# Sums of x on GpSimd between the weight sums, visits kept apart by time, and quad 7 on SP's queue

## The chip, the cores and the metric

The kernel runs on one core of one Trainium2 chip. The metric is the device time of one execution in microseconds (us); smaller is better. Four runs of the kernel before gave 420.64, 421.08, 419.64 and 419.05 us, with a median of 420.14 us. A profile of one execution of each kernel is at hand. Its engines are PE (the matrix engine), PEld (PE's weight loads), DVE (vector), ACT (scalar), POOL (GpSimd) and SP (which only issues DMAs here).

## The reference

Sigmoid attention on 8 batches of 12 heads, 448 positions and head size 64, followed by a gated feed-forward block on the 3584 resulting rows of width 768, with an inner width of 1536:

```python
scores = scale * np.matmul(q, k.transpose(0, 1, 3, 2)) - np.log(S)
attn = 1.0 / (1.0 + np.exp(-scores))          # no softmax: no sum over keys
x = np.matmul(attn, v)                        # then heads side by side: (3584, 768)
g = x @ w_gate
silu = g * (1.0 / (1.0 + np.exp(-g)))
out = (silu * (x @ w_val)) @ w_out
```

## The kernel before, in words

**Attention** is done in 24 *quads*: quad n holds four heads of batch n // 3. Each quad has seven chunks of 64 keys (per head). For one chunk, PE computes the scores of four heads with four small matmuls (L230), ACT applies the sigmoid and writes the tile `pt` (L248, or L245 where the tile is done in halves), and after the seventh chunk PE multiplies by v (`pv`, 28 matmuls at L262). The product lies in PSUM and is copied to two tiles `xT` (L271, L276 on DVE, partly L279 or L284 on ACT). Three quads make the six `xT` tiles of one batch.

**The first feed-forward product** of batch b is `ffn1(b, f)` for f = 0..11: 12 matmuls with 128x448 results (L296), the gate (L314 on ACT, L316 and L320 on DVE) and the tile `hT`. For the last two batches, 6 and 7, it is done another way: `ffn1_pair(j)`, six times, makes seven block products in place of eight (a Strassen-Winograd form, L403), in the order 1, 2, 6, 5, 7, 3, 4. It needs sums of blocks of the weights (`wS`, made by `wx_sums` on POOL, L357, 8 instructions per j) and sums of blocks of x (`xS`, made by `x_sums(i)` for i = 0, 1, 2, L371, 4 instructions each). `x_sums(i)` takes quad 18 + i of batch 6 and quad 21 + i of batch 7, so it can run only when quad 21 + i has its `xT`. Products 6, 5, 7 and 4 of every pair read `xS`.

**The second product** takes two batches at a time: `ffn2` (24 matmuls, L614) for one block of rows, and `ffn2_group(pb, g)` (42 matmuls, L556) for two, again with seven block products, on sums `S` of `hT` (L515) and sums `wT` of w_out (L484). Inside a group, DVE must copy a PSUM bank out (`snap`, L567) before PE may add the next product to it: product 6 is queued behind the snap of product 1.

**PSUM** is a ring of four tiles of two banks; every score tile, `pv`, `ffn1` and group takes the next one.

**The order** of all engines is written out by the program, and no scheduler changes it. A list `units` (L635 on) holds the feed-forward work with estimated durations (FU1 = 2.26 us for an `ffn1`, 3.9 for an `ffn2`, 6.83 for a group). A list `visits` holds the attention work: each quad is visited twice, (n, 0) for chunks 0 to 3 and (n, 4) for chunks 4 to 6; `vtime` gives each visit a due time, spaced by FAST. The loop at L851 walks through the units, adds up their durations in `tcur` and puts a visit ahead of a unit when it is due and when more than one unit stands between it and the visit before (`since > 1`); after LAST, the end of `ffn1(5, 11)`, that second condition is dropped. `pv` of a quad is done in the visit after its second one. A dictionary `plan` (L826) says what is issued behind a visit: `fetch(n)` (q, k and v of quad n loaded through POOL's DMA queue), `casts(n)` (q and k to bf16 on POOL, L181), `trans(n)` (two transposing DMAs on SP's queue, L188), and the sums. `ready(n)` is `casts(n)` and `trans(n)` together. SP's queue also carries the stores of the result (L526). All queues are in order.

`load` puts a quad's q and k into one of four staging tiles; the `casts` of two quads earlier free the tile.

Of the kernel before, what the change touches and what calls it, by code (L numbers as in the profile page):

```python
# [21 lines left out]
def kernel(  # L22
# [10 lines left out]
    nc = tc.nc  # L33
    ctx.enter_context(tc.manual_schedule())

    B, H, S, D = q.shape
# [3 lines left out]
    NJ = H // 4  # L40
    NP = H // 2
    NF = DFF // 128
    NQ = B * NJ
# [9 lines left out]
    stg = ctx.enter_context(tc.tile_pool(name="stg", bufs=4))  # L53
    c16 = ctx.enter_context(tc.tile_pool(name="c16", bufs=4))
# [108 lines left out]
    def load(n, which, eng=None):  # L163
        ramp = 2 * n + (1 - which)
        st = (
            stg.tile([128, 2, S], FP32, tag=f"R{ramp}", bufs=1, name=f"st{which}_{n}")
            if ramp < NR else stg.tile([128, 2, S], FP32, tag="stg", name=f"st{which}_{n}")
        )
        (eng or nc.sync).dma_start(out=st, in_=src_of(n, which))
        qkv_st[(n, which)] = st  # L170

    def load_v(n):
        t = v16p.tile([128, 2, S], FP16, tag="v16", name=f"v16_{n}")
        nc.gpsimd.dma_start(out=t, in_=src_of(n, 2))  # L174
        v16[n] = t
# [157 lines left out]
    def wx_sums(j, room):  # L333

        s = j // FW * 2
        cs = slice(j % FW * 128, j % FW * 128 + 128)
        for kind, w16 in enumerate((wg16, wv16)):
            if room == "stg":
                t = stg.tile([128, 2, S], FP32, tag="stg", name=f"wS{kind}_{j}").bitcast(FP16).rearrange("p a b -> p (a b)")
                t = [t[:, i * 384:(i + 1) * 384] for i in range(4)]  # L340
            else:
                t = []
                for i in range(2):
                    if room == "c16":
                        u = c16.tile([128, C, 2, D], BF16, tag="c16", name=f"wS{kind}_{j}_{i}").bitcast(FP16)
                        u = u.rearrange("p c h d -> p (c h d)")
                    else:
                        u = ptp.tile([128, 2, S], FP16, tag="pt", name=f"wS{kind}_{j}_{i}").rearrange("p a b -> p (a b)")
                    t += [u[:, :384], u[:, 384:768]]
            t = [u.rearrange("p (i n) -> p i n", i=NP // 2) for u in t]  # L350
            a11, a12 = w16[s][:, 0::2, cs], w16[s][:, 1::2, cs]
            a21, a22 = w16[s + 1][:, 0::2, cs], w16[s + 1][:, 1::2, cs]
            if j == 0 and kind == 0:

                nc.gpsimd.tensor_copy(out=t[0][:, 0, :1], in_=hT[(LB // 2 - 1, NF - 1)][:, 1, :1])
            for n, a, b, op in ((1, a21, a22, ADD), (2, t[0], a11, SUB), (3, a11, a21, SUB), (4, a12, t[1], SUB)):
                nc.gpsimd.tensor_tensor(out=t[n - 1], in0=a, in1=b, op=op)  # L357
                wS[(kind, n, j)] = t[n - 1]

    def x_sums(i):  # L360

        t = []
        for n in range(2):
            if i < 2:
                u = v16p.tile([128, 2, S], FP16, tag="v16", name=f"xS{i}_{n}")
            else:
                u = ptp.tile([128, 2, S], FP16, tag="pt", name=f"xS{i}_{n}")
            t += [u[:, 0, :], u[:, 1, :]]
        b11, b12, b21, b22 = (xT[(LB + h, 2 * i + p)] for p in range(2) for h in range(2))
        for n, a, b, op in ((3, b22, b12, SUB), (2, t[2], b11, ADD), (1, b12, b11, SUB), (4, b21, t[1], SUB)):  # L370
            nc.vector.tensor_tensor(out=t[n - 1], in0=a, in1=b, op=op)  # L371
            xS[(n, i)] = t[n - 1]

    def f32_of(tag):
# [290 lines left out]
    FIRST = f1_end[0] - 5.0  # L665
    LAST = f1_end[LB - 1]
    QN = 2 * NJ
    SLOW = 12.2
    FAST = (LAST - 5.5 - (FIRST + 3.5 + 3 * SLOW)) / (NQ - 2 - QN - 3)
    at_end = {(NQ - 2, 4): LAST, (NQ - 1, 0): LAST + FU2, (NQ - 1, 4): LAST + FU2 + FU3}  # L670
    tiles = [(n, c) for n in range(NJ, NQ) for c in range(C)]
    visits = [tiles[:2], tiles[2:4]]
    for i in range(0, len(tiles), C):
        visits += [tiles[i:i + 4], tiles[i + 4:i + C]] if i else [tiles[4:C]]
    vtime = []
    for grp in visits:
        n, c = grp[0]
        b, j = divmod(n, NJ)
# [5 lines left out]
            vtime.append(at_end.get((n, c), FIRST + 3.5 + min(at, 3) * SLOW + max(at - 3, 0) * FAST) - 0.01)  # L684

    def attn_step(group, pvs, how):
        done = list(pvs)
        for part in (group[:2], group[2:]):
            scs = [(n, c, qk_tile(n, c)) for n, c in part]
            rest = [pv(pvs.pop(0), how) for _ in range(len(pvs))]  # L690
            for i, (n, c, sc) in enumerate(scs):

                sig_tile(n, c, sc, split=len(group) == 4 and part[0] == group[0] and i == 1)
            for f in rest:
                f()
        for n in done:
            if n // NJ == B - 1:
                x_sums(n % NJ)

    NPE = 2 * NJ  # L700

# [31 lines left out]
    def fetch(n):  # L733
        load(n, 0, G)
        load(n, 1, G)
        load_v(n)

    def w_out(i):
# [79 lines left out]
    for f, Df in enumerate(early):  # L818
# [7 lines left out]
    plan = {  # L826
        (3, 2): ((casts, 5), (post.append, 4)),
        (3, 4): ((post.append, 5),),
        (4, 0): ((fetch, 6),),
        (4, 4): ((ready, 6),),  # L830
        (5, 4): ((fetch, 7), (w_out, 0)),
        (6, 0): ((ready, 7), (w_out, 1)),
        (6, 4): ((fetch, 8), (w_out, 2)),
        (7, 0): ((ready, 8), (w_out, 3)),
        (7, 4): ((fetch, 9),),
# [8 lines left out]
        if n + 3 < NQ:  # L844
            plan[(n, 4)] += ((fetch, n + 3),)

    plan[(NQ - 1, 0)] = tuple((partial(wx_sums, room=r), j) for j, r in enumerate(("stg", "stg", "c16")))
    plan[(NQ - 1, 4)] = ((partial(wx_sums, room="pt"), 3),)


    seq = []  # L851
    tcur = 3 * FU1
    since = 99
    was, was_args = ffn1, (0, 2)
    for dur, fn, args in units:
        if visits and tcur >= vtime[0] and not (was is ffn1 and was_args[1] == 0) and (vtime[0] < FIRST + 4 or since > 1 or tcur > LAST - 0.1):
# [14 lines left out]
    for fn, args, how in seq:  # L871
        if fn is None:
            pvs, pend = pend, []
            attn_step(args, pvs, how)
            for n, c in args:
                for act, of in plan.get((n, c), ()):
                    act(of)
                if c == C - 1:
                    pend.append(n)
            while post:  # L880
                trans_pe(post.pop())
            continue
# [37 lines left out]
```

## Time and profile before

| what | value |
|---|---|
| median of 4 runs | 420.14 us |
| profiled execution | 420.64 us |
| its span, first to last instruction | 418.3 us |
| PE busy | 401.1 us (96%) |
| DVE, ACT, POOL busy | 266.2, 232.0, 157.6 us |
| mean granted clock of PE | 0.990 |

The profiled execution took 2.34 us more than its span; that part lies outside the first and last instruction. A row of a timeline is: start in us, duration in us, engine, line, operation, tiles, shapes, count, and in brackets the idle time before it with what ended it. A row of a group is the same without a start, and behind the bar the busy time in us, the mean of one in ns, and the idle time before. A row of a stretch gives for each engine its busy time and, in brackets, the number of instructions, then the granted PE clock (1.00 is full), the share of the DMA engines and GB/s. Matmuls overlap (one is shown with about 0.35 us, though the next starts after 0.16 to 0.19 us), so "PE busy" hides short losses; starts of rows are the better measure.

### The profile page before, as it was taken

What the parts mean: (1) busy time and instruction counts of PE and PEld (TensorE: products, weight loads), DVE (VectorE), ACT (ScalarE), POOL (GpSimd) and SP (SyncE); (2) the same over time, 40 slices, a digit from 0 to 9 for tenths busy, and PEclk for the clock granted to TensorE, in tenths of its full rate; (3) what the DMA queues carried; (4) which work ended last, traced back from release to release, by engine and by line L of the source; (5) the groups of instructions that cost most, each with busy time, mean ns of one, the idle gap of its engine ahead of it and who ended that gap; (6) DMA issues with size and microseconds to landing.
All of it is one profiled execution on the core that took longest, in us unless ns stands there. A gap on an engine that the chain in (4) does not pass through costs nothing. (4 is left out here: it accounts for less than half of the span.)

```text
span 418.3 us, 8017 instructions
## 1 busy us (share of the span) xinstructions
PE 401.1 (96%) x3158; PEld 207.5 (50%) x3158; DVE 266.2 (64%) x474; ACT 232.0 (55%) x333; POOL 157.6 (38%) x194
## 2 busy tenths in 40 slices
PE   7799999999999999999999999999987799999995
PEld 3444544445565444454555444445444455555553
DVE  2636647678854545777655455677896646886753
ACT  5976885745415677677304667667772136566100
POOL 3628153334330633330003243200299607996000
PEclk9899999999999999999999999999999989999999
DMA  8999999997779986573226979332012330000125
GB/s 271 244 262 235 213 211 227 120 197 201 204 142 242 205 198 148 100 114 90 55 78 144 250 178 191 55 42 45 3 38 57 96 77 1 1 2 0 39 77 148
DMA packets 59844, 54.38 MB, mean 130 GB/s; under 512 B 35744, under 2 KB 53280, under 8 KB 59808
## 3 DMA queue, kind: packets, MB, share of 16 engines
q0 software_dynamic: 18880, 30.94, 33.9%
q1 hardware_dynamic: 40496, 22.62, 26.9%
q8 instruction: 24, 0.39, 0.4%
q10 hardware_dynamic: 432, 0.33, 0.3%
q14 instruction: 12, 0.10, 0.1%
HBM read 47.19 MB, written 11.01 MB: 139 GB/s over the span
## 5 line engine op out<-in xcount | busy, mean ns | idle before, releaser
L248 ACT ACTIVATE pt<-ps_D,sb_t 128x896 f16<-128x896 f32 x148 | 140.3, 1011 | 79.2 <-PE ps_D L230 78.9
L296 PE MATMUL ps_D<-xT,wg 128*128 128x448 f16 x432 | 95.3, 353 | 0.1
L296 PE MATMUL ps_D<-xT,wv 128*128 128x448 f16 x432 | 94.8, 352 | 0.0
L316 DVE TENSOR_TENSOR t<-ps_D,s 128x448 f16<-128x448 f32 x72 | 44.8, 622 | 62.0 <-ACT s L314 61.9
L181 POOL CAST c<-st 128x896 bf16<-128x896 f32 x41 | 38.2, 944 | 112.9 <-DMA T<-c 60.6
L296 PEld LDWEIGHTS <-wv 128*128 128x128 f16 x432 | 42.2, 98 | 39.5 <-issue 0.4
L296 PEld LDWEIGHTS <-wg 128*128 128x128 f16 x432 | 39.4, 98 | 45.1 <-issue 12.4
L314 ACT ACTIVATE s<-ps_D 128x448 f16<-128x448 f32 x72 | 39.7, 551 | 39.8 <-PE ps_D L296 20.9
L320 DVE SCALAR_TENSOR_TENSOR hT<-ps_D,t 128x448 f16<-128x448 f32 x72 | 45.0, 625 | 7.5
L230 PE MATMUL ps_D<-T,T 64*64 64x448 bf16 x644 | 44.9, 360 | 3.3 <-ACT pt L248 1.2
L556 PE MATMUL ps_D<-wT,S 128*128 128x384 f16 x198 | 35.6, 337 | 5.0 <-DVE osb L567 5.0
L556 PEld LDWEIGHTS <-S 128*128 128x128 f16 x264 | 26.4, 100 | 23.4 <-issue 7.1
L262 PE MATMUL ps_D<-pt,v 64*64 64x448 f16 x672 | 37.1, 358 | 0.5 <-DMA v<-in_v_dram 0.5
L567 DVE TENSOR_SCALAR osb<-ps_D 128x384 f32<-128x384 f32 x43 | 24.0, 557 | 19.6 <-PE ps_D L556 19.3
L174 POOL DMA_DIRECT2D v<-in_v_dram x24 | 17.6, 733 | 49.3 <-PE ps_D L230 47.6
L230 PEld LDWEIGHTS <-T 64*64 64x64 bf16 x644 | 15.2, 106 | 26.6 <-issue 19.4
L271 DVE CAST xT<-ps_D 128x448 f16<-128x448 f32 x24 | 15.0, 624 | 19.0 <-PE ps_D L262 18.7
L573 DVE SCALAR_TENSOR_TENSOR osb<-ps_D,osb 128x384 f32<-128x384 f32 x33 | 18.4, 558 | 13.1 <-PE ps_D L556 12.9
L262 PEld LDWEIGHTS <-v 64*64 64x64 f16 x672 | 19.8, 109 | 13.7 <-issue 1.4
L556 PEld LDWEIGHTS <-hT 128*128 128x128 f16 x198 | 18.9, 98 | 14.2 <-issue 2.1
L276 DVE CAST xT<-ps_D 64x448 f16<-64x448 f32 x40 | 24.9, 621 | 0.6
L614 PE MATMUL ps_D<-wo,hT 128*128 128x384 f16 x144 | 24.2, 326 | 0.5 <-ACT pt L248 0.5
(78 smaller groups left out, 431.0 us busy)
## 6 DMA issues: line engine op xcount, KB each, us to landing
out_dram<-osb SPq DMA_DIRECT2D x52, 192.0 KB, 2.9
st<-in_q_dram POOLq DMA_DIRECT2D x20, 448.0 KB, 4.5
st<-in_k_dram POOLq DMA_DIRECT2D x20, 448.0 KB, 5.6
v<-in_v_dram POOLq DMA_DIRECT2D x24, 224.0 KB, 7.1
wg<-in_moe_w_gate_dram POOLq DMA_DIRECT2D x4, 576.0 KB, 12.0
wv<-in_moe_w_val_dram POOLq DMA_DIRECT2D x4, 576.0 KB, 12.6
wo<-in_moe_w_out_dram POOLq DMA_DIRECT2D x4, 576.0 KB, 10.9
st<-in_q_dram SPq DMA_DIRECT2D x3, 448.0 KB, 7.7
```

Of the source, the lines that this page charges most:

```text
L181: eng.tensor_copy(out=t.rearrange("p c h d -> p h c d"), in_=st.rearrange("p h (c d) -> p h c d", c=C))
L230: nc.tensor.matmul(out=sc[w * 64:(w + 1) * 64, h2, :S], lhsT=kt[r, w * 64:(w + 1) * 64], rhs=qt[r, :, w * 64:(w + 1) * 64], start=True, st ...
L248: nc.scalar.activation(out=pt, in_=sc[:, :, :S], func=SIGM, bias=sb_t, scale=qkscale)
L262: nc.tensor.matmul(out=P[g:g + 64, h2, :S], lhsT=vt[r, h2, c * D:(c + 1) * D], rhs=pt[r, h2, :], start=(c == 0), stop=(c == C - 1),)
L276: done = [nc.vector.tensor_copy(out=o, in_=i) for o, i in halves[how:]]
L296: nc.tensor.matmul(out=D.t[:, i, :S], lhsT=(wg16, wv16)[i][f // FW][:, pr, cs], rhs=xT[(b, pr)], start=(pr == 0), stop=(pr == NP - 1),),
L314: D.read(nc.scalar.activation(out=s16, in_=D.t[:, 0, :S], func=SIGM), 0)
L316: D.read(nc.vector.tensor_tensor(out=t1, in0=D.t[:, 0, :S], in1=s16, op=MULT), 0)
L320: nc.vector.scalar_tensor_tensor(out=hT[(b // 2, f)][:, b % 2, :], in0=D.t[:, 1, :S], scalar=HSC, in1=t1, op0=MULT, op1=MULT),
L556: nc.tensor.matmul(out=D.t[:, bank, :hw], lhsT=l, rhs=B_(i), start=(first and i == 0), stop=(i == HF - 1), skip_group_check=True,),
L567: nc.vector.tensor_scalar(out=o, in0=D.t[:, bank, :hw], scalar1=HREC, scalar2=None, op0=MULT), bank
L614: nc.tensor.matmul(out=D.t[:, half, :hw], lhsT=h[:, m * 128:(m + 1) * 128], rhs=wo16[f // FW][:, f % FW, half * hw:(half + 1) * hw], start ...
```

## The change

The change has four parts.

1. `x_sums` runs on POOL and not on DVE. Its three calls move from the place behind the `pv` to places between the weight sums: behind visit (22, 4) come `wx_sums(0)` and `x_sums(0)`, behind (23, 0) come `x_sums(1)` and `wx_sums(1)`, and behind the last `pv` come `x_sums(2)`, `wx_sums(2)` and `wx_sums(3)`. Tiles that hold the sums are of the same pools as before.
2. A visit is now held back until 3.8 us of estimated unit time have gone by since the visit before, in place of more than one unit, and the exception after LAST is gone.
3. FAST is computed from `LAST - 6.7` and not `LAST - 5.5`, which makes it 11.04 and not 11.13 us per quad. Parts 2 and 3 together move most visits from (9, 4) on by a unit or two towards the start.
4. q and k of quad 7 are loaded on SP's queue (`fetch_sp`) and not on POOL's; its v stays on POOL.

```diff
@@ x_sums
         for n, a, b, op in ((3, b22, b12, SUB), (2, t[2], b11, ADD), (1, b12, b11, SUB), (4, b21, t[1], SUB)):
-            nc.vector.tensor_tensor(out=t[n - 1], in0=a, in1=b, op=op)
+            nc.gpsimd.tensor_tensor(out=t[n - 1], in0=a, in1=b, op=op)
@@
-    FAST = (LAST - 5.5 - (FIRST + 3.5 + 3 * SLOW)) / (NQ - 2 - QN - 3)
+    FAST = (LAST - 6.7 - (FIRST + 3.5 + 3 * SLOW)) / (NQ - 2 - QN - 3)
@@ attn_step
-        done = list(pvs)
...
-        for n in done:
-            if n // NJ == B - 1:
-                x_sums(n % NJ)
@@
+    def fetch_sp(n):
+        load(n, 0)
+        load(n, 1)
+        load_v(n)
@@ plan
-        (5, 4): ((fetch, 7), (w_out, 0)),
+        (5, 4): ((fetch_sp, 7), (w_out, 0)),
...
-    plan[(NQ - 1, 0)] = tuple((partial(wx_sums, room=r), j) for j, r in enumerate(("stg", "stg", "c16")))
-    plan[(NQ - 1, 4)] = ((partial(wx_sums, room="pt"), 3),)
+    wx_stg = partial(wx_sums, room="stg")
+    plan[(NQ - 2, 4)] = ((wx_stg, 0), (x_sums, 0))
+    plan[(NQ - 1, 0)] = ((x_sums, 1), (wx_stg, 1))
@@ the loop over units
-    since = 99
+    last = -9.0
-        if visits and tcur >= vtime[0] and not (...) and (vtime[0] < FIRST + 4 or since > 1 or tcur > LAST - 0.1):
+        if visits and tcur >= vtime[0] and not (...) and (vtime[0] < FIRST + 4 or tcur - last > 3.8):
...
-            since = 0
-        seq.append((fn, args, not visits and since == 1))
+            last = tcur
+        seq.append((fn, args, not visits and tcur - last > 3.8))
...
-        since += dur > 0.0
@@ behind the last visit
             for n in pend:
                 pv(n, 2 if how else 0)
-                if how:
-                    x_sums(n % NJ)
+            if how:
+                x_sums(2)
+                wx_sums(2, "c16")
+                wx_sums(3, "pt")
```

First place: DVE between the last block of `ffn2` of batches 4 and 5 (L627 copies it out) and the start of their first group (L567 and L573 copy a group's products out). Before:

```order
L627 TENSOR_SCALAR osb<-ps_D_101 128x384 x2
L271 CAST xT_2_4161<-ps_D_102 128x448
L276 CAST xT_3_4163<-ps_D_102 64x448
L371 TENSOR_TENSOR xS_1_4184<-xT_3_4163,xT_2_4161 128x448
L371 TENSOR_TENSOR xS_0_4183<-xS_1_4184,xT_2_3698 128x448
L371 TENSOR_TENSOR xS_0_4183<-xT_2_4161,xT_2_3698 128x448
L371 TENSOR_TENSOR xS_1_4184<-xT_3_3700,xS_0_4183 128x448
L567 TENSOR_SCALAR osb<-ps_D_100 128x384
L573 SCALAR_TENSOR_TENSOR osb<-ps_D_100,osb 128x384
```

The same place of the changed kernel:

```order
L627 TENSOR_SCALAR osb<-ps_D_101 128x384 x2
L271 CAST xT_2_4172<-ps_D_102 128x448
L276 CAST xT_3_4174<-ps_D_102 64x448
L567 TENSOR_SCALAR osb<-ps_D_100 128x384
L573 SCALAR_TENSOR_TENSOR osb<-ps_D_100,osb 128x384
```

The four sums have left; the snap of the group (L567) now stands directly behind the casts of quad 22. The same happens in the third group, and the four sums of quad 21 leave the place behind the second visit's casts.

Second place: POOL, from the last weight sum of j = 0. Before, the first weight sum of j = 1 came next; now:

```order
L357 TENSOR_TENSOR wS_0_4090<-wv_0_107,wS_0_4090 128x384
L371 TENSOR_TENSOR xS_1_4096<-xT_1_3998,xT_0_3996 128x448
L371 TENSOR_TENSOR xS_0_4095<-xS_1_4096,xT_0_3458 128x448
L371 TENSOR_TENSOR xS_0_4095<-xT_0_3996,xT_0_3458 128x448
L371 TENSOR_TENSOR xS_1_4096<-xT_1_3460,xS_0_4095 128x448
L371 TENSOR_TENSOR xS_1_4195<-xT_3_4174,xT_2_4172 128x448
L371 TENSOR_TENSOR xS_0_4194<-xS_1_4195,xT_2_3620 128x448
L371 TENSOR_TENSOR xS_0_4194<-xT_2_4172,xT_2_3620 128x448
L371 TENSOR_TENSOR xS_1_4195<-xT_3_3622,xS_0_4194 128x448
L357 TENSOR_TENSOR wS_1_4200<-wg_1_104 128x384
```

Eight sums of x stand between the weight sums of j = 0 and j = 1; the last four stand behind those of j = 1 and ahead of those of j = 2.

Third place: ACT around the end of `ffn1(5, 11)`, with the gates of `ffn1(5, 10)` and `ffn1(5, 11)` (L314) and the sigmoids of quad 22 (L248, L245). Before, all seven score tiles of quad 22 follow the two gates:

```order
L314 ACTIVATE s_3976<-ps_D_100 128x448
L314 ACTIVATE s_3993<-ps_D_102 128x448
L248 ACTIVATE pt<-ps_D_101,sb_t 128x896
L245 ACTIVATE pt<-ps_D_99,sb_t 128x448 x2
L284 CAST xT_1_4042<-ps_D_100 64x448
L248 ACTIVATE pt<-ps_D_102,sb_t 128x896
L248 ACTIVATE pt<-ps_D_101,sb_t 128x896
L248 ACTIVATE pt<-ps_D_99,sb_t 128x896
L248 ACTIVATE pt<-ps_D_100,sb_t 128x896
L248 ACTIVATE pt<-ps_D_102,sb_t 128x896
```

Now the first four stand ahead of the two gates, and three behind them:

```order
L248 ACTIVATE pt<-ps_D_100,sb_t 128x896
L245 ACTIVATE pt<-ps_D_102,sb_t 128x448 x2
L248 ACTIVATE pt<-ps_D_99,sb_t 128x896
L248 ACTIVATE pt<-ps_D_100,sb_t 128x896
L314 ACTIVATE s_4034<-ps_D_102 128x448
L314 ACTIVATE s_4055<-ps_D_101 128x448
L248 ACTIVATE pt<-ps_D_99,sb_t 128x896
L248 ACTIVATE pt<-ps_D_100,sb_t 128x896
L248 ACTIVATE pt<-ps_D_102,sb_t 128x896
```

Visits (22, 0) and (22, 4) no longer stand back to back; two units lie between them.

More of the change, by code (lines that the diff above doesn't have):

```diff
@@ L845 @@
             plan[(n, 4)] += ((fetch, n + 3),)
-    plan[(NQ - 1, 0)] = tuple((partial(wx_sums, room=r), j) for j, r in enumerate(("stg", "stg", "c16")))
-    plan[(NQ - 1, 4)] = ((partial(wx_sums, room="pt"), 3),)
+    wx_stg = partial(wx_sums, room="stg")
+    plan[(NQ - 2, 4)] = ((wx_stg, 0), (x_sums, 0))
+    plan[(NQ - 1, 0)] = ((x_sums, 1), (wx_stg, 1))
     seq = []
     tcur = 3 * FU1
-    since = 99
+    last = -9.0
     was, was_args = ffn1, (0, 2)
     for dur, fn, args in units:
-        if visits and tcur >= vtime[0] and not (was is ffn1 and was_args[1] == 0) and (vtime[0] < FIRST + 4 or since > 1 or tcur > LAST - 0.1):
+        if visits and tcur >= vtime[0] and not (was is ffn1 and was_args[1] == 0) and (vtime[0] < FIRST + 4 or tcur - last > 3.8):
             seq.append((None, visits.pop(0), 0 if fn is ffn1 else 1))
             vtime.pop(0)
-            since = 0
-        seq.append((fn, args, not visits and since == 1))
+            last = tcur
+        seq.append((fn, args, not visits and tcur - last > 3.8))
         was, was_args = fn, args
-        since += dur > 0.0
         tcur += dur
```

## The prediction

> **What bounds the kernel now.** I read the page's busy times first, then the stretches, then PE's waits, then timelines of the stretch that stands out.
>
> ```profile
> PE 401.1 (96%) x3158; PEld 207.5 (50%) x3158; DVE 266.2 (64%) x474; ACT 232.0 (55%) x333; POOL 157.6 (38%) x194
> ```
>
> PE is the bound, so only time in which PE does not issue is to be had. Where that lies, three stretches show:
>
> ```profile
> 30.00:300.00 270.00, 269.90 (x2230) 138.08 (x2232) 172.56 (x317) 163.56 (x226) 81.54 (x102) 1.00 0.75 152
> 300.00:345.00 45.00, 38.11 (x303) 20.63 (x296) 31.19 (x50) 18.69 (x25) 30.05 (x33) 0.96 0.24 62
> 345.00:414.00 69.00, 68.86 (x383) 37.10 (x380) 48.32 (x85) 27.11 (x56) 33.13 (x36) 1.00 0.13 34
> ```
>
> From 30 to 300 us PE is idle for 0.1 us, from 345 on for 0.14 us. Only the 45 us between hold loss: 6.89 us idle and a clock of 0.96. PE's waits name the cause of most of it:
>
> ```profile
> PE ps_D L556 <- DVE osb L567: 5.0, 2, 2.8
> ```
>
> Twice a group's product 6 waited for the snap (L567). DVE's rows show what stood ahead of the snap:
>
> ```profile
> 311.12 0.62 DVE L276 CAST xT<-ps_D 64x448 f16<-64x448 f32 x1
> 311.83 0.50 DVE L371 TENSOR_TENSOR xS<-xT,xT 128x448 f16<-128x448 f16 x1
> ...
> 314.29 1.09 DVE L371 TENSOR_TENSOR xS<-xT,xS 128x448 f16<-128x448 f16 x1
> 315.30 0.55 DVE L567 TENSOR_SCALAR osb<-ps_D 128x384 f32<-128x384 f32 x1
> ```
>
> The four sums of quad 22 fill DVE from 311.83 to 315.30, 3.5 us, with the snap directly behind: without them it starts at 311.8, or when product 1 is there.
>
> **The terms.** Busy time hides pipelined losses, so I take them from starts. The measure without a stall comes from visits and groups that had none:
>
> ```profile
> 281.87 0.76 PE L230 MATMUL ps_D<-T,T 64*64 64x448 bf16 x12
> 282.57 1.31 PE L296 MATMUL ps_D<-xT,wg 128*128 128x448 f16 x6
> 283.71 1.30 PE L296 MATMUL ps_D<-xT,wv 128*128 128x448 f16 x6
> ...
> 287.21 0.57 PE L230 MATMUL ps_D<-T,T 64*64 64x448 bf16 x8
> ...
> 289.42 1.31 PE L296 MATMUL ps_D<-xT,wg 128*128 128x448 f16 x6
> ```
>
> A visit of three tiles takes 282.57 - 281.87 = 0.70 us, one of four tiles with a `pv` 289.42 - 287.21 = 2.21 us, and six matmuls of an `ffn1` 283.71 - 282.57 = 1.14 us (0.19 each). Now quads 22 and 23:
>
> ```profile
> 299.40 0.57 PE L230 MATMUL ps_D<-T,T 64*64 64x448 bf16 x8
> ...
> 304.43 4.06 PE L614 MATMUL ps_D<-wo,hT 128*128 128x384 f16 x24 [0.52 <-ACT pt L248]
> 308.42 0.57 PE L230 MATMUL ps_D<-T,T 64*64 64x448 bf16 x8
> ```
>
> *Visits of quad 22.* (22, 0) and (22, 4), back to back, take 304.43 - 299.40 = 5.03 us, against 2.21 + 0.70: 2.12 lost. PE waits for the ring, which ACT empties:
>
> ```profile
> 302.47 4.60 ACT L248 ACTIVATE pt<-ps_D,sb_t 128x896 f16<-128x896 f32 x5
> ```
>
> Five tiles take 4.60 us, 0.92 each, and PE makes one in 0.23 (0.70 for three). Apart by two `ffn1`, the spacing of the 281.87 and 287.21 rows, which had no stall, each costs its 0.70 and 2.21: gain 2.12. Bounds: 2.12, or 0 if the queue on ACT only moves on to (23, 0). But (22, 4) needs 3 x 0.92 us of ACT and the `ffn2` behind it gives 3.99 us (304.43 to 308.42), so I take 2.12.
>
> ```profile
> 310.94 2.12 PE L556 MATMUL ps_D<-wo,hT 128*128 128x384 f16 x12
> 315.90 3.08 PE L556 MATMUL ps_D<-wT,S 128*128 128x384 f16 x18 [2.83 <-DVE osb L567]
> ```
>
> *Visit (23, 0)* takes 310.94 - 308.42 = 2.52, 0.31 over 2.21. Its third tile needs the ring place that L627 empties on DVE, and the changed order still has six sums of hT (L515) on DVE there; so I leave this 0.31 in.
>
> *The two snaps.* Matmuls of the undisturbed second group give the pace, and behind them the third group begins:
>
> ```profile
> 323.53 3.09 PE L556 MATMUL ps_D<-wT,S 128*128 128x384 f16 x18
> ...
> 326.45 1.14 PE L556 MATMUL ps_D<-wo,S 128*128 128x384 f16 x6
> ...
> 328.50 1.52 PE L262 MATMUL ps_D<-pt,v 64*64 64x448 f16 x28
> ...
> 329.95 2.12 PE L556 MATMUL ps_D<-wo,hT 128*128 128x384 f16 x12
> ```
>
> ```profile
> 334.20 4.76 PE L556 MATMUL ps_D<-wT,S 128*128 128x384 f16 x18 [2.12 <-DVE osb L567]
> ...
> 338.80 1.14 PE L556 MATMUL ps_D<-wo,S 128*128 128x384 f16 x6
> ```
>
> From 323.53 to 326.45 it is 2.92 us for 18, 0.162 each; 12 take 1.95. First group: 315.90 - 310.94 - 1.95 = 3.01 lost. Third group: 334.20 - 329.95 - 1.95 = 2.30 lost. Both go with the sums: ahead of the snap only the casts stay, which by the rows end at 311.74, 1.2 us before product 2 is issued (310.94 + 1.95). What would be late next is the bank of product 2, with its own `put`, which the second group (323.53 on) shows without a wait.
>
> *The clock.* The 18 matmuls from 334.20 take 338.80 - 334.20 = 4.60 where 2.92 is the pace: 1.68 lost. The stretches show why:
>
> ```profile
> 314.15:317.57 3.42, 1.67 (x11) 1.02 (x11) 2.75 (x5) 0.00 (x0) 3.37 (x4) 1.00 0.00 0
> 331.22:334.63 3.41, 1.29 (x9) 0.68 (x7) 3.27 (x6) 0.00 (x0) 1.60 (x2) 1.00 0.30 91
> 334.63:338.05 3.42, 3.42 (x13) 1.66 (x11) 0.95 (x3) 0.00 (x0) 0.00 (x0) 0.50 0.00 0
> ```
>
> After a stretch with 1.29 us of PE work the clock is halved for 3.4 us; after one with 1.67 it is not. With the second wait gone no such stretch is left: gain 1.68. The Trainium skill ("TensorE: Matmul & The Clock Gate", "What's actually happening") says otherwise: the clock halves after at least one idle window of about 3.4 us. PE was never idle that long, so by it this half clock has another cause and the 1.68 may stay. The row at 331.22 speaks for the wait.
>
> *The sums on POOL.* The trace has no sum of x on POOL. The nearest rows are the weight sums, also two f16 tiles to one:
>
> ```profile
> L357 POOL TENSOR_TENSOR wS<-wg,wS 128x384 f16<-128x384 f16 x4 | 3.9, 986 | 0.0
> ```
>
> ```profile
> 300.84 0.25 POOL L355 COPY wS<-hT 128x1 f16<-128x1 f16 x1 [33.26 <-DVE S L515]
> ```
>
> ```profile
> 320.58 0.91 POOL L357 TENSOR_TENSOR wS<-wv 128x384 f16<-128x384 f16 x1
> ...
> 331.77 1.06 POOL L357 TENSOR_TENSOR wS<-wv,wS 128x384 f16<-128x384 f16 x1
> ```
>
> By width, 448/384, a sum costs between 0.91 x 1.17 = 1.06 and 1.06 x 1.17 = 1.24; I take 1.06, since DVE has no two-input sums in most of that time. Twelve add 12.7 us to POOL. Is that covered? POOL starts at L355, about 1.4 us after the visit behind `ffn1(5, 11)` begins (300.84 - 299.40). That visit is now (22, 4). Behind it PE does 0.70, `ffn2` 3.99, (23, 0) 2.52, three groups of 42 x 0.162 = 6.8, (23, 4) 0.70 and the last `pv` 1.45 (329.95 - 328.50): 29.8 us. Product 6 of the first pair comes after 12 matmuls at 0.19, 2.3 us later, and its third matmul first needs `xS` of quad 23: 32.4 - 1.4 = 31 us from L355. POOL needs for the copy, 16 weight sums at 0.986 and ten sums of x: 0.25 + 15.8 + 10.6 = 26.7, or 29.6 at the upper ends 1.06 and 1.24. So it is in time by 1.4 to 4.3 us, and the path pays nothing. The weight sums of j = 2 and 3 follow and are needed two and three pairs (42 x 0.19 = 8 us each) after the first pair's.
>
> *The other moved visits* (from (9, 4) on) lie in the 270 us where PE is full: the same matmuls in another order, 0. A visit that moves by two `ffn1` comes 4 x 1.14 = 4.6 us sooner, and what covers that is the lead of its quad's transposes over its scores; without it PE would wait as in the first rival below.
>
> *Quad 7 on SP.* SP issues its two loads behind both transposes of quad 6. The casts of quad 6's k and of quad 7's k, on POOL, and what a load of this size took on SP:
>
> ```profile
> 51.45 0.94 POOL L181 CAST c<-st 128x896 bf16<-128x896 f32 x1 [0.22 <-DMA st<-in_k_dram]
> ...
> 60.84 0.94 POOL L181 CAST c<-st 128x896 bf16<-128x896 f32 x1 [2.41 <-DMA st<-in_k_dram]
> ```
>
> ```profile
> st<-in_k_dram SPq DMA_DIRECT2D x3, 448.0 KB, 9.1
> ```
>
> k of quad 7 landed by 60.84. On SP it is issued near 54.4 (an estimate: the transpose behind the cast that ends at 52.4, 1.2 us of issue as in the row of L188 below, and two load issues) and lands between 60.8, if the DMA engines set the end, and 54.4 + 9.1 = 63.5. Behind the cast of k wait POOL's loads of quad 8, so its transposes slip by 0 to 2.7 us:
>
> ```profile
> L188 SPq DMA_TRANSPOSE T<-c x2: 1222/1227/1232, 73.2 to 74.6; - x2
> ...
> DMA to landing us min/median/max: 4.9/10.9/16.9
> ```
>
> ```profile
> 94.91 0.57 PE L230 MATMUL ps_D<-T,T 64*64 64x448 bf16 x8
> ```
>
> The second lands at 74.6 + 16.9 = 91.5, and PE wants it at 94.9: a lead of 3.4 us, so 0.7 is left at the worst end. Cost 0.
>
> **Sum.** 2.12 + 3.01 + 2.30 + 1.68 = 9.11. The profiled execution took 420.64 us for a span of 418.3; with 9.1 less that is **411.5 us**. It lay 0.5 above the median of the four runs, 420.14; part of that may be the half clock, which need not fall in every run, so the gain on the median may be nearer 8.6.
>
> **Rivals.**
> - *Quad 8 comes late* (0.13). For: the lead may fall to 0.7, and the second transpose of quad 8 took 16.9 us where the first took 4.9, so it stood behind other transfers. Against: the bytes are the same. If the loads land 2 us later than my upper end, PE waits 1.3 us and may earn a half clock of 1.7 on top: 412.8 to 414.5.
> - *The half clock stays* (0.08), by another cause than the wait: 411.5 + 1.7 = 413.2.
> - *Sums late by a little* (0.07): at 1.4 us per sum of x and 1.06 per weight sum, POOL needs 0.25 + 17.0 + 14 = 31.2 us; each 0.1 us per sum beyond costs the first pair 1 us: 412 to 415.
> - *POOL becomes the bound* (0.04), the slower side. The same kind of sum on DVE shows what a busy other engine does:
>
> ```profile
> L515 DVE TENSOR_TENSOR S<-hT,hT x2: 349/707/1065, 300.3 to 306.4; 128x384 f16<-128x384 f16 x2
> ```
>
> 0.35 us, but 1.07 when POOL worked: three times. If POOL's sums of x are held up so, ten take 10 x 3.2 = 32 us, the first pair comes 32 + 16 - 31 = 17 us late: 428. It turns slower than before from (31 + 9.1 - 15.8) / 10 = 2.4 us per sum. Against: POOL's own rows rise only from 0.91 to 1.06. [...]
> - *The change doesn't reach the wait* (0.04): the snap waits for something else as long, say the store of its tile; then only quad 22's 2.12 and a part of the rest go: 417 to 419.
>
> **Chances.** The forecast has 0.64. Half a per cent, 2.1 us, is about what a measurement of this kernel can tell from no change. Faster by more than that (under 418.0): the forecast, the first three rivals, and some of the last, 0.93; the same 0.03; slower 0.04. The range 409.4 to 415.5 reaches down by the runs' own spread (419.05 is 1.6 below the profiled one) and the 0.31 of visit (23, 0), and up over the first three rivals.
>
> **What would show it.** Right: L371 on POOL near 1.06 us; no wait of PE for L567 near 310 to 330; PE busy over 44 of 45 us from 300 on; no half clock after 30 us; the first `ffn1_pair` 9 us sooner. Wrong: PE waiting in L403 for POOL's L371; PE idle in L230 near 95 us behind a transpose; L371 over 1.4 us; a half clock with no wait ahead of it.

## The result, and the profile after

The changed kernel takes 414.2 us in the median of its 12 executions, the kernel before 420.38 in the median of 17 beside it. The 12 lie in two groups, six from 409.78 to 411.19 and six from 417.22 to 418.51, with nothing between; the profiled execution (418.46 us, span 416.6) is of the upper one, and the ratio that the comparison gives, 0.976 with a 95% interval of 0.972 to 0.979, is of the lower one alone. By the medians of all executions the ratio is 414.2 / 420.38 = 0.985; since the two groups are equally large, this median lies between them, where no execution is. So the change is faster, by 9.7 us in half of the executions (the median of the lower six is 410.7) and by some 2.4 in the others.

What the prediction worked on, the end of the program, came as it said. Three stretches of the profile after:

```profile
30.00:100.00 70.00, 64.23 (x521) 31.31 (x520) 42.70 (x74) 44.38 (x61) 26.61 (x33) 0.95 1.05 183
100.00:300.00 200.00, 199.77 (x1655) 103.18 (x1654) 126.67 (x232) 117.90 (x161) 53.45 (x67) 1.00 0.67 142
300.00:345.00 45.00, 44.62 (x355) 24.14 (x354) 29.23 (x53) 21.08 (x30) 33.71 (x37) 1.00 0.24 63
```

From 300 to 345 us PE is busy for 44.62 of 45 us at the full clock, where it had 38.11 at 0.96. The loss now stands in the first row: 64.23 of 70 us at 0.95, in a stretch of the program where the kernel before lost next to nothing. The starts of the end, on PE's timeline:

```profile
309.17 0.76 PE L230 MATMUL ps_D<-T,T 64*64 64x448 bf16 x12
309.87 4.07 PE L614 MATMUL ps_D<-wo,hT 128*128 128x384 f16 x24
313.87 0.57 PE L230 MATMUL ps_D<-T,T 64*64 64x448 bf16 x8
...
316.44 2.12 PE L556 MATMUL ps_D<-wo,hT 128*128 128x384 f16 x12
318.40 3.09 PE L556 MATMUL ps_D<-wT,S 128*128 128x384 f16 x18
...
332.45 2.12 PE L556 MATMUL ps_D<-wo,hT 128*128 128x384 f16 x12
334.41 3.09 PE L556 MATMUL ps_D<-wT,S 128*128 128x384 f16 x18
...
339.29 0.73 PE L403 MATMUL ps_D<-xT,wg 128*128 128x448 f16 x3
```

In both groups the 18 matmuls follow the 12 after 1.96 us, with no wait: the 3.01 and 2.30 of the snaps are gone. Visit (22, 4) takes 309.87 - 309.17 = 0.70. From L614 to the first pair it is 339.29 - 309.87 = 29.42 us; before it was 340.75 - 304.43 = 36.32, with this first row of the pair:

```profile
340.75 0.73 PE L403 MATMUL ps_D<-xT,wg 128*128 128x448 f16 x3
```

The difference, 6.90, answers to the 3.01 + 2.30 + 1.68 = 6.99 of the sum. The cause is on DVE and POOL:

```profile
317.68 0.56 DVE L567 TENSOR_SCALAR osb<-ps_D 128x384 f32<-128x384 f32 x1 [0.49 <-issue]
```

```profile
334.88 1.03 POOL L371 TENSOR_TENSOR xS<-xS,xT 128x448 f16<-128x448 f16 x1
```

The snap (L567) no longer waits in a queue of sums, and each of the twelve sums of x costs POOL 1.03 to 1.04 us.

What went wrong is near the start. The first row of PE's waits, and PE's timeline around the first tiles of quads 6 and 7:

```profile
PE ps_D L230 <- DMA T<-c: 5.7, 2, 4.2
```

```profile
61.27 1.30 PE L296 MATMUL ps_D<-xT,wv 128*128 128x448 f16 x6
64.04 0.57 PE L230 MATMUL ps_D<-T,T 64*64 64x448 bf16 x8 [1.48 <-DMA T<-c]
...
77.27 1.30 PE L296 MATMUL ps_D<-xT,wv 128*128 128x448 f16 x6
82.77 0.96 PE L230 MATMUL ps_D<-T,T 64*64 64x448 bf16 x8 [4.20 <-DMA T<-c]
...
87.02 1.85 PE L296 MATMUL ps_D<-xT,wg 128*128 128x448 f16 x6
88.70 1.30 PE L296 MATMUL ps_D<-xT,wv 128*128 128x448 f16 x6
```

PE waits for the transposes of quad 6 and then of quad 7. By starts, with 1.23 us from the last six matmuls to a visit that doesn't wait (63.72 - 62.49 at quad 6 in the kernel before), the first costs 64.04 - 61.27 - 1.23 = 1.54 us, the second 82.77 - 77.27 - 1.23 = 4.27. Behind the second the clock is halved:

```profile
77.90:81.30 3.40, 0.67 (x4) 0.14 (x2) 3.23 (x6) 0.11 (x1) 1.71 (x2) 1.00 1.12 288
81.30:84.80 3.50, 2.03 (x24) 1.07 (x28) 0.49 (x1) 1.39 (x2) 3.20 (x5) 0.50 1.18 215
```

The visit from 82.77 takes 4.25 us to the matmuls at 87.02 instead of 2.21, and these 1.68 instead of 1.14: 2.58 lost. Together 1.54 + 4.27 + 2.58 = 8.39 us, and 418.46 - 8.39 = 410.1 lies in the lower group. What is late is on SP's and POOL's timelines:

```profile
51.62 2.67 SPq L188 DMA_TRANSPOSE T<-c  x2
54.40 1.21 SPq L169 DMA_DIRECT2D st<-in_q_dram  x1
```

```profile
52.70 0.72 POOL L174 DMA_DIRECT2D v<-in_v_dram  x1
53.41 0.76 POOL L133 DMA_DIRECT2D wo<-in_moe_w_out_dram  x1
66.34 0.93 POOL L181 CAST c<-st 128x896 bf16<-128x896 f32 x1 [12.16 <-PE ps_D L230]
```

Quad 7's q is issued at 54.40 and its k at 55.72, but the cast of q starts only at 66.34 (before: 57.50) and that of k at 67.47 (before: 60.84). And POOL, which no longer issues q and k there, issues quad 7's v and the first piece of w_out (L133) ahead of them.

### The profile page after: what moved, and what is told of

The parts are those of the page before. It is cut to its first block, busy times and chain, and to the rows that moved or that the text cites. A ratio compares the mean times of both kernels' runs of the same rounds, so it can differ in the third digit from the quotient of the medians.

```text
span 416.6 us, 8018 instructions
## 1 busy us (share of the span) xinstructions
PE 399.6 (96%) x3158; PEld 207.0 (50%) x3158; DVE 260.6 (63%) x463; ACT 231.6 (56%) x332; POOL 167.5 (40%) x204
## 5 line engine op out<-in xcount | busy, mean ns | idle before, releaser
L248 ACT ACTIVATE pt<-ps_D,sb_t 128x896 f16<-128x896 f32 x148 | 140.1, 1017 | 82.0 <-PE ps_D L230 77.3
L314 ACT ACTIVATE s<-ps_D 128x448 f16<-128x448 f32 x72 | 39.5, 549 | 39.8 <-PE ps_D L296 28.6
L567 DVE TENSOR_SCALAR osb<-ps_D 128x384 f32<-128x384 f32 x43 | 24.0, 558 | 20.2 <-PE ps_D L556 19.0
L556 PE MATMUL ps_D<-wT,S 128*128 128x384 f16 x198 | 34.0, 326 | 0.0
L230 PEld LDWEIGHTS <-T 64*64 64x64 bf16 x644 | 15.2, 107 | 31.1 <-issue 18.1
L262 PEld LDWEIGHTS <-v 64*64 64x64 f16 x672 | 20.0, 110 | 14.1 <-issue 2.0
L573 DVE SCALAR_TENSOR_TENSOR osb<-ps_D,osb 128x384 f32<-128x384 f32 x33 | 18.4, 558 | 13.5 <-PE ps_D L556 13.5
L614 PE MATMUL ps_D<-wo,hT 128*128 128x384 f16 x144 | 24.2, 326 | 0.2 <-DVE osb L627 0.2
```

What stands on the lines that cost most here:

```text
L230: nc.tensor.matmul(out=sc[w * 64:(w + 1) * 64, h2, :S], lhsT=kt[r, w * 64:(w + 1) * 64], rhs=qt[r, :, w * 64:(w + 1) * 64], start=True, st ...
L248: nc.scalar.activation(out=pt, in_=sc[:, :, :S], func=SIGM, bias=sb_t, scale=qkscale)
L262: nc.tensor.matmul(out=P[g:g + 64, h2, :S], lhsT=vt[r, h2, c * D:(c + 1) * D], rhs=pt[r, h2, :], start=(c == 0), stop=(c == C - 1),)
L314: D.read(nc.scalar.activation(out=s16, in_=D.t[:, 0, :S], func=SIGM), 0)
L556: nc.tensor.matmul(out=D.t[:, bank, :hw], lhsT=l, rhs=B_(i), start=(first and i == 0), stop=(i == HF - 1), skip_group_check=True,),
L614: nc.tensor.matmul(out=D.t[:, half, :hw], lhsT=h[:, m * 128:(m + 1) * 128], rhs=wo16[f // FW][:, f % FW, half * hw:(half + 1) * hw], start ...
```

## The experiments

The theory at this point: the x sums and the visits give 9 us in every execution; quad 7 on SP takes back 7 to 8 in half of them. The times are medians; the kernel before took 421.8, 420.45 and 421.71 us in the medians beside the three sets.

**Quad 7 back on POOL's queue** (two runs):

```diff
-        (5, 4): ((fetch_sp, 7), (w_out, 0)),
+        (5, 4): ((fetch, 7), (w_out, 0)),
```

> The changed kernel with one line undone: quad 7's q and k are loaded on POOL's queue again. Theory (the gain comes from the end, 300 to 345 us; the loads of quad 7 on SP cost about 7.5 us in some executions: 1.5 at quad 6's scores, 4.2 at quad 7's, 1.8 of half clock): every execution near 410.7, where the faster half of the changed kernel lies, none at 417 to 418, and no wait of PE in L230 for a transpose. Rival A (the moved visits or POOL's other work make those transposes late): still some executions at 417 to 418, with the wait for the transposes. Rival B (the loads on SP are needed, since quad 8 comes late without them): a wait near 95 us at quad 8's scores, 412 or more.

> The changed kernel with quad 7 on POOL's queue once more, beside the others. Theory: all executions between 409.5 and 412, none in the group at 416 to 418, and 0.974 of the kernel before. Rival (the second group is only rarer here): one or two executions at 416 to 418.

410.24 us (409.79 to 411.9, 6 executions; ratio 0.974, 0.971 to 0.976) and 410.83 (410.7 to 411.27, 6 executions; 0.975, 0.971 to 0.978). The upper group is gone in all 12, and PE has no wait for a transpose. With the run that moves w_out (410.46, below) this is the fastest version; what it has over the changed kernel is that the upper group is missing. Its profiled execution, 409.88 us, has the same end as the changed kernel:

```profile
300.97 4.07 PE L614 MATMUL ps_D<-wo,hT 128*128 128x384 f16 x24
...
330.03 0.73 PE L403 MATMUL ps_D<-xT,wg 128*128 128x448 f16 x3
...
332.30 1.30 PE L403 MATMUL ps_D<-xS,wS 128*128 128x448 f16 x6
```

It is 29.06 us from L614 to the first pair, against 29.42 and, before, 36.32; the 0.36 are visit (23, 0), which takes 307.18 - 304.97 = 2.21 here. The two rivals fall: neither the moved visits nor POOL's sums make quad 7's transposes late, and quad 8 doesn't need the loads on SP.

**The changed kernel once more**, beside the second set:

> The changed kernel once more, beside the next three on the same chip. Theory: two groups again, one near 410.7 and one at 417 to 418.5, in the second of which the transposes of quads 6 and 7 land after PE wants them. Rival (a matter of that one chip): only one of the two.

410.1, 410.25, 410.69, 416.1, 417.79, 417.94: two groups again. The profiled execution, 417.94, has the same two waits, 1.10 us at quad 6's scores and 4.39 at quad 7's.

**Quad 7 on SP alone**, in the kernel before:

```diff
-        (5, 4): ((fetch, 7), (w_out, 0)),
+        (5, 4): ((fetch_sp, 7), (w_out, 0)),
```

> The kernel before with quad 7's q and k loaded on SP's queue, nothing else. Theory: some executions at about 420, as before, and some 6 to 8 us slower, 426 to 428, with waits of PE in L230 for the transposes of quads 6 and 7. Rival A (it needs the moved visits too): 420 in all. Rival B (the loads on SP help quad 8): below 420.

Median 422.6 of 13, ten from 419.45 to 423.73 and three from 428.65 to 430.47. The profiled one, 428.65, has the wait:

```profile
PE ps_D L230 <- DMA T<-c: 4.4, 2, 4.0
```

So this part of the change alone costs, in a part of the executions and without the moved visits; it gains nothing in the others (ratio 1.001, 0.998 to 1.004).

**The sums of x alone**, in the kernel before: L371 on POOL, and on POOL's queue in the order of the changed kernel.

```diff
-            nc.vector.tensor_tensor(out=t[n - 1], in0=a, in1=b, op=op)
+            nc.gpsimd.tensor_tensor(out=t[n - 1], in0=a, in1=b, op=op)
...
+    plan[(NQ - 2, 4)] = ((wx_stg, 0), (x_sums, 0))
+    plan[(NQ - 1, 0)] = ((x_sums, 1), (wx_stg, 1))
...
+                x_sums(2)
+                wx_sums(2, "c16")
+                wx_sums(3, "pt")
```

> The kernel before with the sums of x on POOL, interleaved with the weight sums as in the changed kernel; the visits and quad 7 stay as before. Theory, by the terms of the prediction: both waits for the snap go (3.0 and 2.3) and the half clock with the second of them (1.7): 7.0 less, about 413.4; the queue of (22, 4) behind (22, 0) stays. Rival A (the half clock isn't due to that wait): 5.3 less, about 415.1. Rival B (the snap only waits for something else on DVE next): 2 less or nothing.

413.26 us (412.35 to 414.23, 6 executions), ratio 0.980 (0.977 to 0.983): 8.5 less than the 421.8 beside it, 7.1 less than the 420.38 of the first comparison. Rival B falls. In the third group the 18 matmuls take 332.04 - 329.11 = 2.93 us, so the half clock there went with the wait, and rival A falls too. But a half clock is still there in the profiled execution, at another place: in the stretch where (22, 4) stands right behind (22, 0).

```profile
300.52:303.93 3.41, 1.82 (x17) 0.86 (x17) 3.28 (x5) 3.36 (x5) 3.33 (x4) 1.00 0.02 5
303.93:307.34 3.41, 3.41 (x12) 1.63 (x11) 0.27 (x1) 1.97 (x3) 3.33 (x5) 0.50 0.00 0
```

It makes L614 last 308.93 - 303.26 = 5.67 us instead of 3.99, the same 1.68. So from L614 to the first pair it is 333.99 - 303.26 = 30.73 us, only 5.59 less than before: the two waits and the 0.31 of visit (23, 0). The rest of what the medians show isn't in this stretch.

**The visits alone**, in the kernel before:

```diff
-    FAST = (LAST - 5.5 - (FIRST + 3.5 + 3 * SLOW)) / (NQ - 2 - QN - 3)
+    FAST = (LAST - 6.7 - (FIRST + 3.5 + 3 * SLOW)) / (NQ - 2 - QN - 3)
...
-        if visits and tcur >= vtime[0] and not (was is ffn1 and was_args[1] == 0) and (vtime[0] < FIRST + 4 or since > 1 or tcur > LAST - 0.1):
+        if visits and tcur >= vtime[0] and not (was is ffn1 and was_args[1] == 0) and (vtime[0] < FIRST + 4 or tcur - last > 3.8):
...
-        seq.append((fn, args, not visits and since == 1))
+        seq.append((fn, args, not visits and tcur - last > 3.8))
```

> The kernel before with the visits kept apart by time and the other constant of their spacing; the sums of x stay on DVE, quad 7 on POOL's queue. Theory: 2.1 less, about 418.3, from visits (22, 0) and (22, 4) apart, while the snaps still wait. Rival A (with the visits apart quad 22's sums stand elsewhere on DVE and a snap no longer meets them): 4 to 5 less. Rival B (the ring's queue only moves to (23, 0)): 420, as before.

420.66 us against 421.8, ratio 0.998 (0.995 to 1.000): about 1 less, half of what was expected. The visits are apart (L614 comes at 302.10, before at 304.43), but the snaps give it back. PE's timeline and DVE's:

```profile
308.30 2.12 PE L556 MATMUL ps_D<-wo,hT 128*128 128x384 f16 x12
314.09 3.09 PE L556 MATMUL ps_D<-wT,S 128*128 128x384 f16 x18 [3.67 <-DVE osb L567]
```

```profile
303.47 0.36 DVE L515 TENSOR_TENSOR S<-hT,S 128x384 f16<-128x384 f16 x1
303.75 1.07 DVE L515 TENSOR_TENSOR S<-hT,hT 128x384 f16<-128x384 f16 x1
...
313.50 0.54 DVE L567 TENSOR_SCALAR osb<-ps_D 128x384 f32<-128x384 f32 x1
```

The first snap wait costs 314.09 - 308.30 - 1.95 = 3.84 instead of 3.01, the one of the third group 333.41 - 328.14 - 1.95 = 3.32 instead of 2.30. From the sums of hT to the snap DVE pauses once, for 0.42 us, and its two-input sums take 0.95 to 1.09 us each once POOL's weight sums run (from 303.57 on; 0.36 just before): PE, sooner at the group, only waits longer. With the sums of x off DVE the same edit is worth 413.26 - 410.24 = 3.0 us: the 2.12 and, it seems, the half clock of the run before this one. The two parts together bring more than the sum of each alone (1.14 + 8.54 = 9.7 against 421.8 - 410.24 = 11.6).

**Quad 7 on ACT's queue:**

```diff
-        load(n, 0)
-        load(n, 1)
+        load(n, 0, nc.scalar)
+        load(n, 1, nc.scalar)
```

> The changed kernel with quad 7's q and k on ACT's queue instead of SP's, at the same place of the program. Theory A (the loads are late because they stand in SP's queue behind quad 6's two transposes, which land at 63 to 64): on ACT's queue they land before 61, PE doesn't wait for quad 7, all executions near 410.5. Theory B (the DMA engines are full there, whatever the queue): they land at 65 or later on ACT's queue too, with some executions at 417.

416.99 us in the median, three of eight at 409.42 to 410.35 and five at 416.61 to 418.09. In the profiled one ACT issues q at 58.03 (behind ACTIVATEs), 3.6 us later than SP did, and it still lands at the same time, 58.03 + 8.2 = 66.2 (on SP 54.40 + 11.8 = 66.2):

```profile
DMA to landing us min/median/max: 8.2/8.5/8.8
```

This speaks against theory A, and the run with w_out later (below) decides it: there the loads stand at the same place of SP's queue, behind the same transposes, and q lands in 6.1 us. The Trainium skill ("DMA: Bandwidth & Descriptors", "Issuing engines are not separate DMA queues") says that transfers issued by different engines run on the same 16 DMA engines and interleave there; the same landing at 66.2 from both queues agrees with it.

**Quad 7 on SP, ahead of quad 6's transposes:**

```diff
-        (4, 4): ((ready, 6),),
-        (5, 4): ((fetch_sp, 7), (w_out, 0)),
+        (4, 4): ((fetch_sp, 7), (ready, 6)),
+        (5, 4): ((load_v, 7), (w_out, 0)),
```

(In this kernel `fetch_sp` has only the loads of q and k.)

> The changed kernel with quad 7's q and k on SP's queue still, but ahead of quad 6's transposes instead of behind them; v of quad 7 and the first piece of w_out stay where they are. Theory A (it is the place behind the transposes): the loads are issued about 15 us sooner, near 40, land before 56, and all executions are near 410.5. Theory B (the bytes are in the way of others there): quad 6's loads, which take 12 us without them, land later and PE waits for the transposes of quad 6, by 1 to 3 us, with a half clock in some: 412 to 416.

410.77, 411.21, 412.86, 412.9, 414.21, 417.92. The loads land by 47.4, but the rest moves: the cast of quad 6's own k starts 2.5 us later (54.29, in the changed kernel 51.82), and quad 7's transposes, issued at 57.6 and 59.3, take 13.5 and 18.1 us among w_out and quad 8. Neither theory as written: no wait for quad 6 in the profiled execution, and yet up to 417.9.

**The first piece of w_out behind quad 7's casts**, quad 7 on SP as in the change. By the code this piece is 3 x 128 rows of 768 float32, 1.18 MB read.

```diff
-        (5, 4): ((fetch_sp, 7), (w_out, 0)),
-        (6, 0): ((ready, 7), (w_out, 1)),
+        (5, 4): ((fetch_sp, 7),),
+        (6, 0): ((ready, 7), (w_out, 0), (w_out, 1)),
```

> The changed kernel, quad 7's q and k on SP's queue, but the first piece of w_out (1.18 MB) behind quad 7's casts on POOL instead of ahead of them. Theory C (what makes quad 7 late is that v and this piece, no longer behind q and k on POOL, are issued 1 to 2 us ahead of them and share the same DMA engines): q lands near 60 to 61, the transposes of quad 7 are issued by 62, no wait of PE for them, all executions near 410.5. Theory A (SP's queue, behind quad 6's transposes): q lands near 66 as before, some executions at 417.

410.46 us (409.93 to 410.69, 6 executions; ratio 0.973, 0.970 to 0.977), none in the upper group; if half of the executions still fell into it, six without one would be a chance of 1 in 64. POOL's timeline, with w_out behind quad 7's casts (60.24 and 61.38), and the landing of the two loads here and in the changed kernel (in this order):

```profile
62.26 1.52 POOL L133 DMA_DIRECT2D wo<-in_moe_w_out_dram  x2
```

```profile
DMA to landing us min/median/max: 5.7/5.9/6.1
```

```profile
DMA to landing us min/median/max: 11.6/11.7/11.8
```

With quad 7 on SP, issued at 53.95 behind the same two transposes, q lands in 6.1 us instead of 11.8 in the profiled executions, and w_out is all that the edit moved. A stretch of the DMA engines shows the same, from 56 to 60 us, first of the changed kernel, then of this one:

```profile
56.00:60.00 4.00, 4.00 (x31) 1.83 (x30) 1.49 (x3) 3.50 (x5) 0.00 (x0) 1.00 1.41 91
```

```profile
56.00:60.00 4.00, 4.00 (x31) 1.83 (x30) 1.35 (x3) 3.50 (x5) 0.00 (x0) 1.00 1.06 278
```

With the piece of w_out among the transposes the DMA engines are busier (1.41 against 1.06) and move a third of the bytes (91 against 278 GB/s).

**The first piece of w_out ahead, quad 7 on POOL:**

```diff
-        (5, 4): ((fetch_sp, 7), (w_out, 0)),
+        (5, 4): ((w_out, 0), (fetch, 7)),
```

> The changed kernel with quad 7's q and k on POOL's queue, but the first piece of w_out issued ahead of them there. Theory C (order of the bytes): q of quad 7 lands at 64 or later and there are executions at 416 to 418 again, though no load of quad 7 is on SP. Theory A (SP's queue): 410.3, as with quad 7 on POOL's queue.

412.6 us (411.06 to 414.74, 6 executions), some 2 us over the two kernels beside it (410.46, 410.83), with nothing at 416 to 418. In the profiled execution q of quad 7 lands at 61.6, not at 64 or later, and PE waits for quad 6 alone:

```profile
64.60 0.57 PE L230 MATMUL ps_D<-T,T 64*64 64x448 bf16 x8 [0.99 <-DMA T<-c]
```

Theory C as written falls: w_out ahead of the loads isn't enough to make quad 7 late. In the profiled executions quad 7 came late, by 4.0 to 4.4 us, only with both, w_out ahead and the loads on SP or ACT. The 2 us are, in the profiled execution, a half clock within the first 20 us (PE's last matmuls ahead of quad 6 start at 62.31, with quad 7 ahead of w_out at 61.17) and this wait. The wait isn't tied to the order either: two kernels with w_out behind quad 7 on POOL's queue have it too, the visits alone (0.81) and the kernel of the last experiment below (1.18):

```profile
63.81 0.57 PE L230 MATMUL ps_D<-T,T 64*64 64x448 bf16 x8 [1.18 <-DMA T<-c]
```

**The sums of quad 23 eight weight sums later on POOL**, quad 7 on POOL's queue:

```diff
-                x_sums(2)
                 wx_sums(2, "c16")
+                x_sums(2)
```

> The changed kernel with quad 7 on POOL's queue, and the sums of x of quad 23 one place later on POOL, behind the eight weight sums of j = 2. By the trace of the run with quad 7 on POOL's queue they have 5.3 us to spare (second sum ends at 327.3, the third matmul of product 6 is at 332.6), and eight weight sums take 7.2 us. Theory: PE waits 1.9 us at the first pair for the second sum: 412.2, or 413.9 in the executions in which the whole wait lies in one stretch of the clock and a half clock follows. Rival (something else hides it): 410.3, as without.

411.67 us (410.9 to 411.93, 5 executions), 0.8 to 1.4 more than without, in other sets; the lower group of the changed kernel in the same set has 410.25 as its median.

```profile
335.75 3.19 PE L403 MATMUL ps_D<-xS,wS 128*128 128x448 f16 x16 [1.73 <-POOL xS L371]
```

The wait is 1.73 us (expected 1.9), and no half clock follows in the profiled execution. What POOL had to spare is real and is 5 to 6 us.

**The sums of x not between the weight sums**, quad 7 on POOL's queue: each `x_sums` where DVE had it, `plan` and the end as in the kernel before.

```diff
-    plan[(NQ - 2, 4)] = ((wx_stg, 0), (x_sums, 0))
-    plan[(NQ - 1, 0)] = ((x_sums, 1), (wx_stg, 1))
+    plan[(NQ - 1, 0)] = tuple((partial(wx_sums, room=r), j) for j, r in enumerate(("stg", "stg", "c16")))
+    plan[(NQ - 1, 4)] = ((partial(wx_sums, room="pt"), 3),)
```

> The changed kernel with quad 7 on POOL's queue, and on POOL the sums of x where DVE had them, right behind their quad's scores: those of quad 23 behind all 32 weight sums. Theory: the second sum of quad 23 ends near 343 (xS of quad 22 at 312, 32 weight sums at 0.90, two sums of 1.03), PE wants it at 332.6, so it waits 10.5 us, and a half clock of 1.7 follows: about 422, slower than the kernel before. Rival (the order on POOL is of no weight, only that the sums leave DVE): 410.3.

424.32 us (423.4 to 425.27, 10 executions) against 421.71, ratio 1.007 (1.004 to 1.010): the same move of the sums, slower than the kernel before.

```profile
346.01 5.65 PE L403 MATMUL ps_D<-xS,wS 128*128 128x448 f16 x16 [10.84 <-POOL xS L371]
```

The wait is 10.84 us (expected 10.5). The clock takes more than the 1.7 expected: the 16 matmuls last until 351.50, 5.49 us instead of 16 x 0.19 = 3.04, so 2.45. 10.84 + 2.45 = 13.3, and the kernel is 424.32 - 410.83 = 13.5 over the one with the order of the change. The profiled execution, 424.97, has the 1.18 us at quad 6 besides.

## Why the prediction was right, and where it was wrong

Faster was right, and 414.2 lies in the range; but 411.5 was meant for every execution, and no execution of the first comparison lies between 411.2 and 417.2. That the median lies in the range is luck: it is the middle of two groups of six, and with seven executions in the upper one it would have been above 417. The mechanism forecast for the end of the program holds, and the lower group, 410.7, is what it gives; one term, quad 7 on SP, was put at nothing and was not.

- *The two snaps, 3.01 + 2.30, and the clock, 1.68.* Right: 6.99 expected between L614 and the first pair, 6.90 measured. The rival by which the half clock stays has fallen for this place: with the wait gone the stretch runs at 1.00.
- *Visits of quad 22 apart, 2.12.* Right within the whole change (0.70 for (22, 4), as worked out), but not a gain of its own: alone it brings about 1 us, since the snaps wait longer. The prediction summed the terms as if each stood alone; that was safe only because the sums left DVE in the same change.
- *Visit (23, 0), 0.31 left in.* Right in this execution: 316.44 less the visit's start, 313.87, is 2.57 (before 2.52). In the run with quad 7 on POOL it is 2.21, so this loss isn't always there.
- *The sums on POOL, 1.06 each, in time by 1.4 to 4.3 us.* 1.03 to 1.04 measured; the second sum of quad 23 ends at 335.91 and its matmul, by the 2.65 us that the run with quad 7 on POOL has from the pair's start (330.03 to 332.68), is due at 341.9: 6 us to spare. Two experiments confirm that the place on POOL carries it: 7.2 us later there costs 1.7, and behind all weight sums 10.8.
- *The other moved visits, 0.* Right: 199.77 of 200 us busy from 100 to 300.
- *Quad 7 on SP, 0.* Wrong: 8.39 us in the profiled execution and nothing in the lower group. (A wait like the 1.54 at quad 6's scores among them stands also in two kernels with quad 7 on POOL, above; the other 6.85 don't.) Three things in this step failed. The landing of k was bounded by 54.4 + 9.1 = 63.5, with 9.1 from a row of loads on SP at another place; k was issued at 55.72, took 11.6 and landed at 67.3. The lead was read for quad 8 alone, because POOL's loads of quad 8 wait behind the cast; but quad 7's own transposes wait for the same cast. These are rows of the kernel before, the transpose of quad 7's k on SP and the scores on PE:

```profile
L188 SPq DMA_TRANSPOSE T<-c x1: 1231/1231/1231, 61.8 to 61.8; - x1
...
DMA to landing us min/median/max: 10.4/10.4/10.4
```

```profile
78.18 0.57 PE L230 MATMUL ps_D<-T,T 64*64 64x448 bf16 x8
```

  It landed at 61.8 + 10.4 = 72.2, 6.0 us ahead of PE. In the changed kernel the cast of k is 6.6 us later and the transpose is issued at 68.6, 6.8 later; and it takes 14.1 us, 3.7 more:

```profile
DMA to landing us min/median/max: 4.6/9.3/14.1
```

  So it lands at 82.7, where PE has waited 4.27 us. And the step looked at what waits behind the late cast, not at what steps forward on POOL when the loads leave: v and the piece of w_out. With this piece later the loads on SP cost nothing in six executions; ahead on POOL it didn't make quad 7 late, so it takes both. Quad 8, the rival named for this place, was not late: PE's two waits are those of quads 6 and 7.
- *The total.* 418.46 less the 8.39 is 410.1, 1.4 below the forecast. Some 1.2 of that is a half clock in the first 20 us of the profiled execution of before, which the forecast took for its base and the profiled execution after doesn't have:

```profile
13.78:17.19 3.41, 3.41 (x38) 1.51 (x31) 0.79 (x3) 2.66 (x4) 1.95 (x3) 0.50 1.29 212
```

The last matmuls ahead of quad 6's scores start 1.2 us later before than after (61.27, above), at a place up to which PE's work is the same in both:

```profile
62.49 1.30 PE L296 MATMUL ps_D<-xT,wv 128*128 128x448 f16 x6
```

Open: why half of the executions of the changed kernel escape the late transposes. Of these none was profiled; the experiments show what takes the upper group away, not what decides between the groups in one execution. Why the DMA engines move so few bytes with w_out among the transposes is not settled either, nor what makes quad 6's transposes late. By itself this piece isn't it: with quad 7 loaded ahead of the transposes it was issued 1.79 us behind the first of them (55.89 - 54.10), just as in the changed kernel (53.41 - 51.62), and the second landed 6.5 us after its issue, not 10.9.

## What to carry to other kernels

When a load is moved to another queue, two things have a new time: the load, and everything that was behind it and now goes ahead; read the lead of each consumer of both, the moved load's own first. An operation put on a second engine is free only up to the moment its result is wanted: here, moved off DVE, the same 12 sums are worth 7 to 8.5 us between the weight sums, and behind them they make the kernel 13.5 us slower, slower than before. Gains read from one queue's stalls don't add: with DVE still the last to arrive, PE's earlier arrival became a longer wait, and paid only when DVE's work had gone too.

## What the hardware showed that was not expected

**The clock goes by a grid of time.** The half clocks begin at edges of one grid of 3.41 us within an execution, and what counts is how much PE worked in one square of it. The prediction had 1.29 us of work followed by a half clock and 1.67 not; the runs add 0.67 (after, 77.90) and 1.82 (the sums alone) followed by one, and a wait of 3.67 us that cost no clock, where before one of 2.12 did. It is the one before 314.09 in the run of the visits alone, and it lies on both sides of an edge:

```profile
308.98:312.39 3.41, 1.45 (x9) 0.76 (x8) 3.29 (x4) 2.06 (x3) 3.33 (x4) 1.00 0.42 105
312.39:315.80 3.41, 1.71 (x11) 1.05 (x11) 2.74 (x5) 0.00 (x0) 3.41 (x4) 1.00 0.00 0
315.80:319.21 3.41, 3.41 (x25) 1.92 (x27) 1.74 (x5) 0.00 (x0) 3.33 (x5) 1.00 0.00 0
```

Behind 0.67 the half clock lasted for two squares (to 88.2); in the first of them PE worked for 2.03 us, mostly on 64-row matmuls. So a stall costs a further 1.4 to 2.6 us (333.41 of the visits alone: 337.73 - 333.41 - 2.92 = 1.40; after: 2.58) or nothing, by where it falls; this is, likely, a part of why executions of one kernel differ by some us. The Trainium skill ("TensorE: Matmul & The Clock Gate", "What's actually happening") has a free-running window of 3413 ns, which agrees; its half rate after at least one idle window doesn't, since half-busy windows were enough here. Busy time alone isn't the measure: 1.82 us, mostly of 64-row matmuls, was followed by a half clock and 1.45 us of 128-row ones was not. What PE counts is open.

**DVE pays for POOL's work, POOL little for DVE's.** In the kernel before, the last of the four sums of a quad took DVE 1.09 us at 314.29 (a row of the prediction), while POOL worked, and the same sum of the next quad 0.38, after POOL's row of weight sums had ended at 332.83:

```profile
333.30 0.38 DVE L371 TENSOR_TENSOR xS<-xT,xS 128x448 f16<-128x448 f16 x1
```

Not every sum pays so much: the first one of a quad took 0.50 to 0.89 us beside POOL. POOL's weight sums up to 333 us, two of them in the rows of the prediction, go from 0.91 to 1.06 at most.
